# A gated spectral mixer with product-key experts: another source for the tiles of D, rows copied two steps behind their transposes, one store of u, wider score pairs, and one-hots issued one at a time

## The chip, the cores and the metric

The kernel runs on one core of a Trainium2 chip. Its time is the device time of one execution in microseconds (us). Three runs of the kernel before gave 785.18, 786.75 and 787.69; their median is 786.75. One further execution was profiled and took 783.8.

## The reference

There are S = 2048 tokens of D = 640 columns. The result is y = g\*a + (1-g)\*b with a gate g for each token.

```python
g = sigmoid((x * gate_w).sum(-1))
# a: Fourier mixing over both axes, as dense products
ar = x @ Wd_re.T ; ai = x @ Wd_im.T
a  = Ws_re @ ar - Ws_im @ ai                    # 2048 x 2048 by 2048 x 640
# b: H = 32 heads with product keys, E = 16 keys a side, 256 experts
q  = einsum("nd,dhc->nhc", x, w_q)              # two halves of 128
s1 = q[..., :128] @ k1.T ; s2 = q[..., 128:] @ k2.T
#   the two best of s1 and of s2, the two best of their four sums,
#   g2 = softmax over these two
ue, ve = u[top_e], v[top_e]
b  = einsum("nhk,nhk,nhkd->nd", g2, gelu(einsum("nd,nhkd->nhk", x, ue)), ve)
```

All inputs and the output are fp32. The best-two choice needs the scores at nearly full precision.

## The kernel before

**Products in three parts.** TensorE works on pairs of tiles h and l, where h is a value rounded to the fp32r type and l is the rest. `split(f, h, l, eng)` (L128 to L132) makes them: ScalarE copies f to h, and VectorE or GpSimd (the argument `eng`) subtracts h from f. `mm3` (L134 to L138) adds h by h, h by l and l by h in one PSUM bank. Nearly all of TensorE's time goes into such triples.

**The Fourier part.** The program takes the sequence product first: Ws times x, for real and imaginary parts, in four column groups of 512, each with 16 tiles of W down the sequence. One such tile is a *piece*, with five triples for the five blocks of x (`seq_piece`). The order is all of the real part, the imaginary group 2, then 56 units of a fast 2-by-2 scheme for the imaginary groups 0 and 1 (`quad_step`; the units a11, s1, a12, s2, s4, s3, a22, some of which need sums of W and sums of x), and last the imaginary group 3. Together these are the NPC = 152 pieces of the *first product*. Its results go through ST, a ring of five staging tiles, are multiplied by g or -g on VectorE ("gate products", L227, L293, L307), and are stored in `pd`. The *second product* multiplies them by the D-side matrices Wd and by v, in two rounds of 42 steps, by the same kind of scheme. Its right-hand tiles are called DD (h and l of Wd), `ts` (h and l of sums of Wd) and `vs` (v); DD takes the place of WU, the weights of the score stage, in memory.

**W's lead.** Tiles of W are loaded some five pieces ahead (`wf`) and split three pieces ahead into WS, a ring of four pairs: at piece n the program issues the split of piece n+3, whose buffer piece n-1 has used. In the score stage GpSimd makes the subtraction; from N1 on VectorE does.

**The score stage** lies over pieces N0 to N1. There are eight pairs of token tiles, and a pair takes five pieces: `score_half` behind four of them (15 triples that make the 512 score columns of half a tile), `u_pair` behind the last (the products of x with u, a gelu on ScalarE, and the stores into `actd`). After `u_pair` stands `split_xT`, which makes xh and xl of the next pair on ScalarE and GpSimd; there is one pair of buffers for them. Over the same pieces run the sums of W (`sums_load` to `sums_last`, stored in `sd`) and of x (`x_load` to `x_store`, stored in `td`) that the quad units read back.

**Background work.** `Pump` holds generators of small pieces of VectorE work (the choice of the best two, `topk`, L600 to L621, and the experts). Each triple on TensorE calls `run_bg(0.68)`, which adds share x 0.68 us of credit; generators are advanced until the credit is spent, and each yields the microseconds that it used. A negative yield means "nothing now" and sets the credit to zero. Work with a fixed cost elsewhere takes credit away. `space(f, us)` is a second list: its entries are called in turn, each when the given time has passed since the one before. Through it go the *rows*: expert numbers and weights of a token tile are transposed by three DMAs on SP's queue (`load_rows`), and one step later copied into ROWS by ScalarE (`put_rows`, L685; for the last four tiles by GpSimd). `at(n, f)` puts f behind piece n.

**The experts.** For each of 32 *chunks* of tokens VectorE builds one-hot factors from ROWS (`build`: three operations, L821 to L823, of 2048 elements for a group of two chunks, of 1024 for one), TensorE multiplies them (`use`), ScalarE copies the result to `cd` (L830), and for every fourth chunk `cd` is stored in `gd` by two DMAs on ScalarE's queue (L836). The second product reads `gd`. Groups are double up to eight pieces before the end of the first product, and single from there.

**D's tiles.** `load_dd` and `split_dd` load Wd in five parts of two tiles from N1 on, into the buffers of xf, xh and xl, and split the ten tiles into DD on ScalarE and VectorE. Later `load_dt` loads the same rows of Wd again (and v), from 17 pieces before the second product; `make_sums` and `split_sums` make the sums and split them. The two meet in one place, `t_sum`, which lets one sum's h and l overwrite a quarter of DD (n == 3).

What the order of instructions on an engine is, the program writes out itself: it runs under a manual schedule, and an instruction waits only for its operands and buffers. W, rows, sums and D's parts are loaded over SP's queue; ScalarE's queue carries the stores of `actd`, `gd`, `pd` and the output; GpSimd's queue loads `tq` (the x side of the quad units) and stores part of `pd`.

## Time and profile before

| | |
|---|---|
| median of three runs | 786.75 us |
| the profiled execution | 783.8 us, span 782.0 us |
| TensorE (PE) busy | 762.8 us, 98% of the span |
| VectorE (DVE) busy | 582.5 us, 74% |
| GpSimd (POOL) busy | 358.8 us, 46% |
| ScalarE (ACT) busy | 304.5 us, 39% |
| mean granted clock of TensorE | 0.995 |

In the trace the score stage runs from about 160 to 430 us and the first product ends at about 622 us. A row of the view of instructions gives the start, the duration, the engine, the line, output and input, and in brackets the time that the instruction waited, with what released it. A row of the view of waits gives the waiting engine and tile, what released it, the total wait, the number of waits and the longest. A row of a window gives its bounds and length, then the busy time of PE, PEld, DVE, ACT and POOL with the number of instructions, then the granted clock, the share of the DMA engines and the GB/s. A row of the grouped view gives line, engine, operation and tiles, the busy time and the mean of one in ns, and the idle time before them. ACTq and SPq are the DMA issues on the queues of ScalarE and SyncE.

### The profile page before, as it was taken

To read this page: it belongs to the slowest core of one execution; us is meant where nothing else is said; L and a number is where in the kernel's file an instruction comes from. 1 tells how busy PE (TensorE), PEld (TensorE's weight loads), DVE (VectorE), ACT (ScalarE), POOL (GpSimd) and SP (SyncE) were. 2 spreads that over 40 slices of the span, in tenths; PEclk is the share of its full clock that TensorE was granted. 3 is DMA by queue.
4 is the path that set the end of the run, shared out by engine and by line. 5 is a ranking of instruction groups with operands and counts; after the bars stand their busy time and mean duration, and the time that the engine had idled before them with its cause. 6 is when DMAs were issued, how large, how long until landed. Compare 5 with 4: busy or idle time off the path is not lost.

```text
span 782.0 us, 12300 instructions
## 1 busy us (share of the span) xinstructions
PE 762.8 (98%) x4568; PEld 612.8 (78%) x4568; DVE 582.5 (74%) x676; ACT 304.5 (39%) x505; POOL 358.8 (46%) x279
## 2 busy tenths in 40 slices
PE   9999999999999989998999999999999999999997
PEld 6777677888888878886888877778778788788886
DVE  7641121398999999999999985878689878748761
ACT  5344323232225342444425454434324543543342
POOL 5433224466755575575755024222003465577253
PEclk9999999999999999999999999999999999999999
DMA  9977996646445555636755579898736687676421
GB/s 346 355 264 192 308 342 209 220 145 199 144 168 167 201 184 175 206 109 203 268 164 163 203 235 266 279 297 254 240 104 209 200 273 235 203 256 215 125 63 69
DMA packets 111453, 165.29 MB, mean 211 GB/s; under 512 B 35040, under 2 KB 50528, under 8 KB 111392
## 3 DMA queue, kind: packets, MB, share of 16 engines
q1 hardware_dynamic: 80656, 136.30, 53.0%
q10 hardware_dynamic: 27088, 15.87, 6.6%
q0 software_dynamic: 3648, 12.32, 4.8%
q8 instruction: 36, 0.59, 0.3%
q14 instruction: 25, 0.20, 0.1%
HBM read 126.17 MB, written 36.71 MB: 208 GB/s over the span
## 4 chain that ended last, share of the span: by engine, by line
PE 64%; DVE 20%; DMA 6%; issue 3%; SPq 2%; POOL 2%; ACT 2%; ACTq 0%; DVEq 0%; POOLq 0%
PE b L136 20%; PE b L137 19%; PE b L138 19%; DVE ew L611 3%; PE b L490 2%; DVE rr L615 2%; DVE mm L609 2%; SPq L677 2%; DVE ew L613 2%; DVE ew L618 2%; DVE sc L620 2%; DMA wf<-in_wsim 1%; DMA gd<-cd 1%; DVE WS L132 1%; DVE ST L227 1%
## 5 line engine op out<-in xcount | busy, mean ns | idle before, releaser
L136 PE MATMUL b<-WS,X 128*128 128x512 f32 x555 | 220.1, 397 | 2.8 <-ACT WS L131 1.3
L137 PE MATMUL b<-WS,X 128*128 128x512 f32 x555 | 217.2, 391 | 2.8 <-DVE WS L132 2.7
L138 PE MATMUL b<-WS,X 128*128 128x512 f32 x555 | 216.5, 390 | 0.0
L132 POOL TENSOR_TENSOR WS<-wf,WS 128x512 fp32r<-128x512 f32 x72 | 108.2, 1509 | 124.1 <-ACT WS L131 113.5
L131 ACT ACTIVATE WS<-wf 128x512 fp32r<-128x512 f32 x152 | 94.0, 628 | 102.3 <-PE b L138 43.1
L136 PEld LDWEIGHTS b<-WS,X 128*128 128x128 f32 x555 | 104.3, 188 | 33.5 <-issue 7.8
L137 PEld LDWEIGHTS b<-WS,X 128*128 128x128 f32 x555 | 104.4, 188 | 24.9 <-DVE WS L132 4.6
L138 PEld LDWEIGHTS b<-WS,X 128*128 128x128 f32 x555 | 104.4, 188 | 22.2
L596 ACT ACTIVATE sc<-b 128x512 f32<-128x512 f32 x32 | 19.5, 609 | 134.9 <-PE b L138 134.9
L132 DVE TENSOR_TENSOR WS<-wf,WS 128x512 fp32r<-128x512 f32 x80 | 53.8, 695 | 23.2 <-ACT WS L131 23.1
L136 PE MATMUL b<-WU,xh 128*128 128x512 f32 x160 | 63.0, 394 | 2.8 <-ACT xh L131 2.8
L138 PE MATMUL b<-WU,xl 128*128 128x512 f32 x160 | 63.2, 395 | 2.3 <-POOL xl L132 2.3
L132 POOL TENSOR_TENSOR WS<-ra,WS 128x512 fp32r<-128x512 f32 x40 | 58.1, 1469 | 15.5 <-ACT WS L131 14.1
L137 PE MATMUL b<-WU,xh 128*128 128x512 f32 x160 | 62.8, 392 | 0.0
L275 POOL DMA_DIRECT2D tq<-td x32 | 17.5, 549 | 85.3 <-PE b L138 46.1
L131 ACT ACTIVATE WS<-ra 128x512 fp32r<-128x512 f32 x56 | 34.9, 631 | 54.8 <-PE b L138 33.4
L132 POOL TENSOR_TENSOR WP<-ra,WP 128x512 fp32r<-128x512 f32 x20 | 32.2, 1624 | 46.0 <-ACT WP L131 44.1
L505 DVE TENSOR_TENSOR WU<-b,WU 128x512 fp32r<-128x512 f32 (+1 forms) x16 | 7.9, 491 | 58.2 <-ACT WU L504 58.2
L611 DVE TENSOR_TENSOR ew<-sc,mm 128x1024 f16<-128x1024 f32 x32 | 49.7, 1552 | 1.1
L609 DVE TENSOR_REDUCE mm<-sc 128x64 f32<-128x1024 f32 x32 | 38.9, 1215 | 13.6 <-ACT sc L596 13.0
L996 DVE TENSOR_TENSOR ra<-ra 128x512 f32<-128x512 f32 x48 | 44.6, 980 | 3.5 <-POOL WP L132 3.2
L615 DVE TENSOR_REDUCE rr<-ew 128x64 f16<-128x1024 f16 x32 | 39.0, 1219 | 1.0
(161 smaller groups left out, 1453.7 us busy)
## 6 DMA issues: line engine op xcount, KB each, us to landing
wq<-in_wq SPq DMA_DIRECT2D x32, 640.0 KB, 7.1
ra<-pd SPq DMA_DIRECT2D x70, 256.0 KB, 3.9
wf<-in_wsre SPq DMA_DIRECT2D x63, 256.0 KB, 5.2
wf<-in_wsim SPq DMA_DIRECT2D x56, 256.0 KB, 4.4
sa<-in_wsim SPq DMA_DIRECT2D x32, 256.0 KB, 3.0
sd<-sa SPq DMA_DIRECT2D x32, 256.0 KB, 2.0
tq<-td POOLq DMA_DIRECT2D x32, 256.0 KB, 5.3
wf<-sd SPq DMA_DIRECT2D x32, 256.0 KB, 4.6
```

The lines of the kernel that those rows point to most:

```text
L131: nc.scalar.activation(h, f, AF.Copy)
L132: eng.tensor_sub(l, f, h.bitcast(F32))
L136: nc.tensor.matmul(o, wh, ah, start=first, stop=False, skip_group_check=more)
L137: nc.tensor.matmul(o, wh, al, start=False, stop=False, skip_group_check=more)
L138: nc.tensor.matmul(o, wl, ah, start=False, stop=last, skip_group_check=more)
L275: nc.gpsimd.dma_start(t.bitcast(F32), td[k, :, ("s1", "s3", "a22", "s2").index(what)])
L490: nc.tensor.matmul(ps[32 * j:32 * j + 32, :HALF], kp[:, 8 * G // H, r, :], w[:, j], start=(r == 0), stop=(r == 1))
L596: nc.scalar.activation(scs[i].rearrange("p h e -> p (h e)")[:, c], ps, AF.Copy)
L609: nc.vector.tensor_reduce(m, sc, op=OP.max, axis=AX.X)
L611: nc.vector.tensor_tensor(eq, sc, m[:, :, None].to_broadcast([P, HH, E]), op=OP.is_equal)
L615: nc.vector.tensor_reduce(r, eq, op=OP.max, axis=AX.X)
L996: nc.vector.tensor_add(take((b, o, k)) if f is not None else raw[b, o, k], raw[b, o, k] if f is None else f, raw[b, what, k])
```

## The change

Five things are different, and some small ones go with them.

1. `load_dd` and `split_dd` are gone. `make_sums` splits DD's h and l out of the tile that `load_dt` has loaded for the sums: one ScalarE copy and one VectorE subtraction of 2 x 640 columns for each of the five tiles. `load_dt` runs a piece later from the third tile on.
2. Rows are copied two steps behind their transposes, with 8 us between steps; for the last four tiles one step behind with 6 us. There are three buffers for `rt`.
3. u's two results are stored by one DMA instead of two. Except where the next piece is the last of its column group, this store is issued behind the next piece, after the split of the next pair's x.
4. A pair of score tiles gets a sixth piece every second time: the stage is 44 pieces long instead of 40.
5. The three operations of a one-hot group are yielded singly, so that other work may stand between them. A pause no longer forfeits the credit that is left (up to 2.4 us are kept). A group whose result goes into a fresh `cd` is used 12 us after the issue of the last store into `gd` at the earliest, and while the later buffers don't exist yet, a group is used 8 us after it was built.

Smaller: the h parts of x's sums are stored a piece or two earlier than the l parts; `sd`'s last store stands at the start of the next pair; the gate rows and one result row share a buffer with `sx`; one pair of quad units changes places, so that s2 ends a unit earlier; `tq`'s first loads come a piece later; the credit's share in the quad units and behind is 1.12 instead of 1.1.

```diff
+QUNITS[5 * HN - 3:5 * HN - 1] = QUNITS[5 * HN - 2:5 * HN - 4:-1]
...
             if c is None or c < 0:
-                self.credit = 0.0
+                self.credit = 0.0 if c is None else min(self.credit, 2.4)
...
 def load_rows(a):
-            t = p2.tile([P, 3, P], F16, name="rt", bufs=2)
+            t = p2.tile([P, 3, P], F16, name="rt", bufs=3)
...
+        lag, gap = (1, 6.0) if b == NT // NB - 1 else (2, 8.0)
         def step(a):
             if a < NB:
                 got[a] = load_rows(a)
-            if a:
-                put_rows(a - 1, got.pop(a - 1))
-        for a in range(NB + 1):
-            bg.space(lambda a=a: step(a), 5.0 if a and b == NT // NB - 1 else 8.0)
+            if a >= lag:
+                put_rows(a - lag, got.pop(a - lag))
+        for a in range(NB + lag):
+            bg.space(lambda a=a: step(a), gap)
...
+    def apart(n):
+        return n if pieces[n + 1][2] == NT - 1 else n + 1
 def u_pair(p):
         nc.scalar.activation(act, ps, AF.Gelu_apprx_tanh)
-        for n in range(2):
-            nc.scalar.dma_start(actd[n][:, 2 * p * P:2 * (p + 1) * P], act[:, n])
+        def put_act():
+            nc.scalar.dma_start(actd[:, :, 2 * p * P:2 * (p + 1) * P].rearrange("n p t -> p n t"), act)
+        n = N0 + 5 * p + p // 2 + 4
+        if apart(n) == n:
+            put_act()
+        else:
+            at(n + 1, put_act)
...
     for p in range(NP):
-        n = N0 + 5 * p
+        n = N0 + 5 * p + p // 2
...
+        at(apart(n + 4), x_high, p)
...
-    N1 = N0 + 5 * NP
-    at(N1, x_store, HN - 1)
+    N1 = N0 + 5 * NP + NP // 2
+    at(N1 - 1, sums_last, HN - 1)
+    at(N1 - 1, x_store, HN - 1)
...
 def build(g, c, s, n, us):
             nc.vector.tensor_tensor(pt, row(0), wt, op=OP.is_equal)
+            yield us
             nc.vector.tensor_tensor(qt, row(1), wt, op=OP.is_equal)
+            yield us
             nc.vector.tensor_tensor(pt, pt, row(2), op=OP.mult)
+            yield us
...
 def use(group):
+            while group[0][1] % 4 == 0 and bg.now < put[0] + 12.0 and not ending:
+                yield -1.0
...
-                    if p3 is None:
-                        yield 3.0
+                    while p3 is None and bg.now < built + 8.0:
+                        yield -1.0
...
-                build(g, c, s, k)
-                yield (1.1 if not last_part else 1.65) * 2 if k == 1 else 3.6
+                yield from build(g, c, s, k, 1.2 if k == 2 else 1.1 if last_part else 0.75)
...
-    def load_dd(m):
-    def split_dd(m, a):
...
 def make_sums(k):
         bg.credit -= 2.3
+        if k < KD:
+            split(f, DD[:, :, 0, k], DD[:, :, 1, k], nc.vector)
+            bg.credit -= 1.5
...
-        at(NPC - 17 + 2 * k, load_dt, k)
+        at(NPC - 17 + 2 * k + (k > 1), load_dt, k)
...
-        share = 0.95 if n < N1 else 1.0 if n < Q0 + 8 else 1.1
+        share = 0.95 if n < N1 else 1.0 if n < Q0 + 8 else 1.12
```

The order that comes of it, at three places. In these rows a number behind x counts equal instructions in a row, and a line number is that of the kernel in question: the split is L131 and L132 before, L134 and L135 in the changed kernel.

ScalarE at the end of the fifth score pair (the gelu of u, L718 before and L731 now, the store of u, the split of the next pair's x), before:

```order
L131 ACTIVATE ST<-sx 128x512 x2
L718 ACT_TABLE_LOAD
L718 ACTIVATE ST<-b_2525 128x512
L720 DMA actd<-ST 128x256 x2
L131 ACTIVATE xh<-xf 128x640 x2
L131 ACTIVATE WS<-wf 128x512 x2
L596 ACTIVATE sc<-b_2626 128x512
```

and of the change:

```order
L134 ACTIVATE ST<-sx 128x512 x2
L731 ACT_TABLE_LOAD
L731 ACTIVATE ST<-b_2561 128x512
L134 ACTIVATE xh<-xf 128x640 x2
L134 ACTIVATE WS<-wf 128x512
L734 DMA actd<-ST 128x2x256
L134 ACTIVATE WS<-wf 128x512
L694 ACTIVATE rows_1188<-rt 128x384
```

The store has moved from ahead of the split of x to behind it and one split of W; at the third and the sixth pair it still stands right behind the gelu.

VectorE in the quad units (one-hots L821 to L823, the split's subtraction into WS, the gate product into `wrow`, an addition L289), before:

```order
L132 TENSOR_TENSOR WS<-wf,WS 128x512 x3
L821 TENSOR_TENSOR hot_4059<-rows_1189,wtab_144 128x2048
L822 TENSOR_TENSOR hot_4059<-rows_1189,wtab_144 128x2048
L823 TENSOR_TENSOR hot_4059<-hot_4059,rows_1189 128x2048
L307 SCALAR_TENSOR_TENSOR wrow<-b_3730,grow 128x512
L289 TENSOR_TENSOR ST<-ST,b_3884 128x512
L132 TENSOR_TENSOR WS<-wf,WS 128x512
```

and of the change, where the one-hots are L847, L849 and L851, the gate product into the shared buffer is L316 and the addition L298:

```order
L135 TENSOR_TENSOR WS<-wf,WS 128x512 x4
L847 TENSOR_TENSOR hot_4144<-rows_1188,wtab_143 128x2048
L849 TENSOR_TENSOR hot_4144<-rows_1188,wtab_143 128x2048
L851 TENSOR_TENSOR hot_4144<-hot_4144,rows_1188 128x2048
L847 TENSOR_TENSOR hot_3567<-rows_1188,wtab_143 128x2048
L135 TENSOR_TENSOR WS<-wf,WS 128x512 x2
L849 TENSOR_TENSOR hot_3567<-rows_1188,wtab_143 128x2048
L851 TENSOR_TENSOR hot_3567<-hot_3567,rows_1188 128x2048
L316 SCALAR_TENSOR_TENSOR rest<-b_3615,rest 128x512
L298 TENSOR_TENSOR ST<-ST,b_3834 128x512
L135 TENSOR_TENSOR WS<-wf,WS 128x512
```

Three one-hots stood ahead of the two result operations before; now there are four one-hots, two splits, two one-hots and then these operations.

VectorE at the end of the first product (the last sums of Wd and v, L943 to L947 before and L942 to L946 now; the splits into `vs` and `ts`; what follows are the operations on `ra` of the second product), before:

```order
L132 TENSOR_TENSOR WS<-wf,WS 128x512
L943 TENSOR_TENSOR tf<-dt 128x512
L944 SCALAR_TENSOR_TENSOR tf<-tf,dt 128x256
L945 TENSOR_TENSOR tf<-tf 128x256
L946 TENSOR_TENSOR tf<-dt 128x256
L947 TENSOR_TENSOR tf<-dt 128x128
L132 TENSOR_TENSOR vs<-dt,vs 128x1280
L132 TENSOR_TENSOR ts<-tf,ts 128x256
L132 TENSOR_TENSOR vs<-tf,vs 128x256
L132 TENSOR_TENSOR ts<-tf,ts 128x128
L1032 TENSOR_SCALAR ra<-ra 128x512
```

and of the change:

```order
L135 TENSOR_TENSOR DD<-dt,DD 128x2x640
L135 TENSOR_TENSOR WS<-wf,WS 128x512
L135 TENSOR_TENSOR ts<-tf,ts 128x256
L135 TENSOR_TENSOR DD<-tf,DD 128x256
L135 TENSOR_TENSOR ts<-tf,ts 128x128
L135 TENSOR_TENSOR WS<-wf,WS 128x512
L851 TENSOR_TENSOR hot_3567<-hot_3567,rows_1189 128x1024
L847 TENSOR_TENSOR hot_3567<-rows_1189,wtab_143 128x1024
```

The subtraction for DD stands ahead of a split of W, and behind the last split of W come one-hots of single groups, the last of them (L849 and L851) behind the splits into `vs` and `ts`.

More of the change, by code (lines that the diff above doesn't have):

```diff
@@ L57, in __init__ @@
         self.clock = 0.0
+        self.now = 0.0
     def space(self, f, us):
@@ L65, in tick @@
         self.clock += us
+        self.now += us
         if self.apart and self.clock >= self.apart[0][1]:
@@ L215, in gated_mix_kernel, with row_tile @@
     p3, last_part, ending, share = None, False, False, 0.95
-    grow, staged = {}, {}
+    grow, staged, rest = {}, {}, []
+    def row_tile(q):
+        if q < NC:
+            return pools[-1].tile([P, TC], F32, name="grow", tag="grow")
+        if not rest:
+            rest.append(pa.tile([P, 2, TC], F32, name="rest", tag="C"))
+        return rest[0][:, 0]
     def load_row(q):
-        grow[q] = pools[-1].tile([P, TC], F32, name="grow", tag="grow")
+        grow[q] = row_tile(q)
         nc.sync.dma_start(grow[q], gdr[q % NC * TC:(q % NC + 1) * TC].partition_broadcast(P))
@@ L319, in q_post @@
         elif what == "a12":
-            f = p3.tile([P, TC], F32, name="wrow")
+            f = rest[0][:, 1]
             at(n, w_out, 0, f)
@@ L731, in x_load @@
     def x_load(k):
-        sa["x"] = p2.tile([P, 2, TC], F32, name="sx")
+        sa["x"] = pa.tile([P, 2, TC], F32, name="sx", tag="C")
         nc.sync.dma_start(sa["x"], xn[k::HN, :, :4 * P].rearrange("a p d -> p a d"))
@@ L758, in x_split, with x_high @@
             split(f, sa["h"][n], f.bitcast(F32R), nc.gpsimd)
+    def x_high(k):
+        for n in range(2):
+            nc.sync.dma_start(td[k, :, 2 * n:2 * n + 2, 0], sa["h"][n].bitcast(F32).rearrange("p (j c) -> p j c", j=2))
     def x_store(k):
@@ L762, in x_store @@
             return
-        for n in range(2):
-            nc.sync.dma_start(td[k, :, 2 * n:2 * n + 2, 0], sa["h"][n].bitcast(F32).rearrange("p (j c) -> p j c", j=2))
         nc.sync.dma_start(td[k, :, :, 1], sa["x"].rearrange("p n (j c) -> p (n j) c", j=2))
@@ L837, in sums @@
                                         cd[g][n::2, :, n, :])
+                put[0] = bg.now
             if c == 15:
@@ L1173, in gated_mix_kernel @@
             bg.add(experts(), late=True)
-        if HOT and p3 is None and len(rowed) == NT and not grow:
+        if HOT and p3 is None and len(rowed) == NT:
             p2_stack.close()
```

40 lines of the change are left out of this document (12 added, 28 removed).

## The prediction

> **What bounds the kernel now.** I read the page first (shares of the engines, granted clock), then the waits of TensorE, then its busy time in stretches of 20 us, and last the instructions around each gap.
>
> ```profile
> PE 762.8 (98%) x4568; PEld 612.8 (78%) x4568; DVE 582.5 (74%) x676; ACT 304.5 (39%) x505; POOL 358.8 (46%) x279
> ```
> ```profile
> PE b L136 <- ACT xh L131: 2.8, 2, 1.6
> PE b L137 <- DVE WS L132: 2.7, 3, 1.4
> PE b L849 <- ACT cd L830: 2.6, 2, 1.9
> ...
> PE b L136 <- DVE ST L309: 1.3, 1, 1.3
> ```
> ```profile
> 280.00:300.00 20.00, 17.38 (x70) 13.59 (x69) 19.48 (x21) 6.86 (x10) 10.07 (x6) 0.91 0.66 219
> 340.00:360.00 20.00, 17.52 (x91) 14.46 (x89) 19.52 (x16) 7.23 (x12) 13.87 (x11) 1.00 0.42 128
> 460.00:480.00 20.00, 18.55 (x142) 14.84 (x142) 12.22 (x19) 6.35 (x11) 7.79 (x10) 1.00 0.95 285
> 480.00:500.00 20.00, 18.48 (x141) 14.43 (x140) 14.71 (x18) 8.62 (x15) 6.36 (x9) 1.00 0.92 277
> 500.00:520.00 20.00, 18.86 (x203) 14.57 (x202) 16.34 (x23) 8.93 (x15) 4.54 (x8) 1.00 0.85 252
> 540.00:560.00 20.00, 18.10 (x255) 14.29 (x254) 14.03 (x16) 5.64 (x11) 3.44 (x6) 0.91 0.80 254
> 560.00:580.00 20.00, 18.71 (x203) 14.76 (x203) 16.78 (x22) 6.33 (x11) 0.55 (x1) 1.00 0.61 179
> 600.00:620.00 20.00, 19.26 (x208) 15.73 (x208) 18.59 (x31) 11.86 (x27) 8.11 (x9) 1.00 0.67 189
> ```
>
> TensorE has work in 98% of the span and the change neither adds nor removes a matmul, so all that can be won is what these rows lack of 20 us: 2.62, 2.48, 1.45, 1.52, 1.14, 1.90, 1.29 and 0.74 us, 13.1 together. Two rows also show a granted clock of 0.91, that is 1.8 us of full-speed work lost in each. The ceiling is thus 16.7 us, or 2.1% of the span. The waits name four different releasers: no single cause is behind it, so I take the gaps one by one.
>
> **The score stage (two gaps).** The rows of ScalarE around them:
>
> ```profile
> 278.05 0.94 ACT L718 ACTIVATE ST<-b 128x512 f32<-128x512 f32 x1
> 281.95 2.15 ACTq L720 DMA_DIRECT2D actd<-ST  x2
> 284.15 1.36 ACT L131 ACTIVATE xh<-xf 128x640 fp32r<-128x640 f32 x2 [5.16 <-DMA wf<-in_wsre]
> ```
> ```profile
> 357.59 1.37 ACT L131 ACTIVATE xh<-xf 128x640 fp32r<-128x640 f32 x2 [6.99 <-DMA actd<-ST]
> ```
>
> The gelu ends at 279.0, but the two stores of u are issued only at 281.95 and 283.8, each after the landing of an earlier transfer, and the split of the next pair's x stands behind them on the same queue. TensorE waits for it. The change issues one store, and in six of eight pairs behind the split and one piece later (its order is shown above); for the other two pairs the store still comes first, but there the transposes lie a step away. Its own wait then holds up only splits of W, which have a lead: the ring is four buffers, so up to three pieces. I count both gaps and the lost clock as won: 2.62 + 2.48 + 1.8 = 6.9. If they stay, nothing of that comes.
>
> A copy of rows, too, waits on that queue now:
>
> ```profile
> L685 ACT ACTIVATE rows<-rt 128x384 f16<-128x384 f16 x12 | 23.4, 1950 | 11.4 <-DMA rt<-gs 11.3
> ```
>
> Two steps behind instead of one, with 8 us between steps, the 11.3 us of waiting should go; they lie beside matmuls in all but the gaps above, so I add nothing for them.
>
> Spreading the pairs over 44 instead of 40 pieces adds no matmul, but it sets what VectorE must do in that stage against more time:
>
> ```profile
> 160.00:430.00 270.00, 264.88 (x1271) 222.69 (x1270) 261.18 (x242) 99.33 (x139) 168.77 (x113) 0.99 0.55 179
> 430.00:570.00 140.00, 133.90 (x1301) 106.45 (x1300) 112.96 (x155) 60.63 (x101) 27.79 (x41) 0.99 0.80 250
> 570.00:622.00 52.00, 49.98 (x463) 40.49 (x462) 47.43 (x78) 21.34 (x48) 14.45 (x16) 1.00 0.56 167
> ```
>
> VectorE is busy 261 of 270 us there. Without the two gaps the stage would be 263 us long and VectorE next to bind; four pieces more (15 matmuls each, one every 0.227 us by the rows of 552 us further down, so 3.4 us a piece) make it 276.7, VectorE at 94%. So the cover for the 6.9 us is the spreading. It is paid for later: the same four pieces no longer stand between the score stage and the products.
>
> **D's parts from the other tiles.** Removed after the score stage: ten loads of 320 KB, ten ScalarE copies, and ten VectorE subtractions.
>
> ```profile
> L132 DVE TENSOR_TENSOR DD<-draw,DD 128x640 fp32r<-128x640 f32 x10 | 8.2, 818 | 0.0
> ```
> ```profile
> 458.31 3.09 DVE L227 SCALAR_TENSOR_TENSOR ST<-ST,grow 128x512 f32<-128x512 f32 x5
> 461.32 0.82 DVE L132 TENSOR_TENSOR DD<-draw,DD 128x640 fp32r<-128x640 f32 x1
> 462.06 0.68 DVE L132 TENSOR_TENSOR WS<-wf,WS 128x512 fp32r<-128x512 f32 x1
> ```
>
> The gap at 461 (1.45) is this: five gate products, then a part of D, then the split that TensorE waits for. Before it stands another part of D. Without them, and with the gate products still in a stretch of whole pieces, 1.45 goes to zero. The work comes back as five subtractions of 1280 columns in the last 14 pieces before the second product; the trace prices them at 8.2 us in all (two of 818 ns each), and their ScalarE copies beside them have room (21.3 of 52 us busy). What it displaces is costed under the end, below.
>
> **One-hots singly, and the new waits in the list of background work.**
>
> ```profile
> 480.91 2.10 ACTq L836 DMA_DIRECT2D gd<-cd  x2
> 483.06 1.09 ACT L286 ACTIVATE ST<-b 128x512 f32<-128x512 f32 x2 [4.05 <-DMA rt<-gs]
> ...
> 554.60 0.60 ACT L830 ACTIVATE cd<-b 128x512 f32<-128x512 f32 x1 [7.53 <-DMA gd<-cd]
> ```
> ```profile
> DMA to landing us min/median/max: 4.5/5.5/11.1
> ```
>
> At 553 the copy into cd waits 7.53 us for the landing of gd, read from the same cd, and the splits of W stand behind it. The change lets a first group be used only 12 us after the issue; the slowest landing took 11.1. So 1.90 goes, and with it the slow clock (1.8): the rows of the matmuls show when it came.
>
> ```profile
> 552.73 0.39 PE L137 MATMUL b<-WS,X 128*128 128x512 f32 x1
> 552.95 0.39 PE L138 MATMUL b<-WS,X 128*128 128x512 f32 x1
> ```
> ```profile
> 556.82 0.63 PE L136 MATMUL b<-WS,tq 128*128 128x512 f32 x1
> 557.25 0.63 PE L137 MATMUL b<-WS,tq 128*128 128x512 f32 x1
> ```
>
> Before the gap one matmul starts every 0.22 to 0.23 us, after it every 0.43, and the idle time between was only 1.90 us; the 2.48 us at 356 left the clock at 1.00, so whether a gap costs clock too is not in its length alone. [...]
>
> At 483 it is gd's issue that waits, 4.05 us, behind a transpose's landing. In the new order the first gd comes after more loads; the background list also pauses there. I take the 1.52 as won; bounds 0 to 1.52.
>
> What one-hots cost in the products is shown by the gap at 507:
>
> ```profile
> 502.83 1.22 DVE L821 TENSOR_TENSOR hot<-rows,wtab 128x2048 f16<-128x2048 f16 x1
> ...
> 507.43 0.69 DVE L132 TENSOR_TENSOR WS<-wf,WS 128x512 fp32r<-128x512 f32 x1
> ```
>
> From 502.83 to 507.43, 4.6 us (three one-hots and two additions), no split comes, and TensorE lacks 1.14 in that slice. The change puts splits between one-hots at most places, but not at this one: the order has four one-hots in a row (4 x 1.14 = 4.6), two splits, then two one-hots and two additions (3.5). The first costs 1.1 again, the second between 0 and 1.8, since the lead is used up; I take 0.9, so this place gets dearer by 0.9. The gap at 572 (1.29, L309 in the waits) keeps a chunk of the same length, three one-hots and two additions; I leave it.
>
> **The end of the first product.** From 570 to 622 VectorE is free for 4.6 of 52 us. The order adds 8.2 of D there, and one-hots for 12.8 instead of 11.0 us (two groups of 3 x 1.22 and three half groups, against three groups): 5.4 more than there is. The lead of up to three pieces takes most of that. But a half group is now used two microseconds before the end of the stage, and its last two one-hots stand behind the last sums: TensorE waits between 0 and 5.4 there; I take 2.0, since VectorE starts the stretch with some pieces in hand. Four single uses instead of one double add 0.5 by my estimate from the 0.74 of the slice that now holds two in a row.
>
> The other edits (x stores a piece earlier, sd's last store a piece later, shared buffers for rows, s2 ending a unit earlier, dt a piece later, share 1.12) move transfers whose landings are not named in the waits; they cost nothing while the lead of the splits holds.
>
> **Sum.** Won 6.9 + 1.45 + 1.52 + 1.90 + 1.8 = 13.6; lost 0.9 + 2.0 + 0.5 = 3.4; net 10.2. The profiled execution took 783.8 us (span 782.0 and 1.8 around it), so 773.6 for one like it. The median of the runs is 786.75, 2.95 above it; with that, 776.5.
>
> **Rivals.** *VectorE sets the pace after the score stage.* From 430 to 622 it is busy 160.4 of 192 us, 83.5%, and loses cover when pieces move forward. If it can't get denser, only the score stage's 6.9 remain, less up to the 3.4: 780 to 783. For it: 47 of 52 at the end; against: 96.7% in the score stage hardly hurt. 0.20.
> *More goes than I count*: the gaps at 507, 572 and 610 as well, 13.6 + 1.14 + 1.29 + 0.74 = 16.8: 770. For it: more splits stand between one-hots. 0.10.
> *The landing waits only change place*: the store of u, or a late copy of rows, still stops ScalarE ahead of what TensorE needs. The 6.9 stay and the 3.4 eat the rest up to 3.3: 783 to 787. Against it: the split now precedes the store. 0.12.
> *Slower: the end is bound by VectorE, with GpSimd beside it.*
>
> ```profile
> 586.54 0.42 DVE L945 TENSOR_TENSOR tf<-tf 128x256 f32<-128x256 f32 x1
> 586.87 0.96 DVE L946 TENSOR_TENSOR tf<-dt 128x256 f32<-128x256 f32 x1
> ```
>
> Like shapes take 0.42 alone and 0.96 beside GpSimd's part of the sums. If all of D's 8.2 stretched so, 10.5 more, the stretch would be 16 us late, and a slow clock 1.8 more: against the 12.2 won elsewhere (13.6 less 0.9 and 0.5) that is 5.5 slower, 792. [...] It decides from a lateness of 14.6 on (12.2 and the 2.4 of a measurable loss). 0.08.
>
> **Chances.** My forecast 0.50, its own range 773 to 780. A measurement tells 0.3% from no change, 2.4 us here. Faster (under 784.4): 0.50 + 0.20 + 0.10, less the upper edge of the second case, 0.03: 0.77. Same: that edge and most of the third rival, 0.14. Slower 0.09. The range that leaves out two in ten or less, from the rival with more to the third rival: 769.5 to 786.
>
> **What would show it.** Right: no wait of TensorE for xh or xl, the clock at full in the slices around 285 and 556, no wait for cd after a gd store. Wrong: waits for WS by VectorE in the last ten pieces, waits of L849's successor for hot, a slow clock at new places. The forecast fails if VectorE's share from the score stage's end to the second product stays at 83.5%.

## The result, and where the time went

The changed kernel takes 776.65 us (median of four runs, 776.48 to 777.08), the kernel before 785.96 (four runs, 784.50 to 787.69). The ratio is 0.9881, with a 95% interval of 0.9859 to 0.9904: faster by 1.2%. On a second chip the same comparison gave 777.97 against 786.17, a ratio of 0.9900 (0.9877 to 0.9923). The forecast was 776.5 with a range of 769.5 to 786.0. Runs over 1.5% slower than the fastest of the same kernel on the same chip are left out of the ratios, here and below; that takes 9 of the 29 runs of the kernel before on the chip of e9 to e12.

The profiled execution of the changed kernel took 777.08 us, its span is 775.3. From its page, the shares of the engines:

```profile
PE 760.8 (98%) x4568; PEld 612.3 (79%) x4568; DVE 577.3 (74%) x673; ACT 303.4 (39%) x502; POOL 367.1 (47%) x283
```

The waits of TensorE (what it waited for, the total, the number, the longest):

```profile
PE b L881 <- ACT cd L859: 3.0, 1, 3.0
PE b L881 <- DVE hot L851: 2.7, 1, 2.7
PE b L140 <- DVE WS L135: 1.2, 1, 1.2
...
PE b L139 <- ACT ST L1130: 0.9, 1, 0.9
```

and the windows of 20 us that answer to those shown of before, with two at the end of the first product:

```profile
280.00:300.00 20.00, 20.00 (x93) 16.68 (x92) 19.48 (x26) 7.03 (x11) 11.38 (x8) 1.00 0.57 188
340.00:360.00 20.00, 19.93 (x103) 16.77 (x102) 18.38 (x14) 11.89 (x17) 18.41 (x12) 1.00 0.43 144
460.00:480.00 20.00, 20.00 (x192) 16.05 (x191) 12.55 (x16) 8.91 (x15) 7.33 (x9) 1.00 0.96 270
480.00:500.00 20.00, 18.68 (x183) 14.66 (x170) 18.93 (x22) 9.03 (x15) 5.78 (x7) 1.00 0.84 272
...
540.00:560.00 20.00, 20.00 (x331) 15.83 (x330) 16.39 (x19) 7.51 (x13) 0.55 (x1) 1.00 0.78 245
...
580.00:600.00 20.00, 17.00 (x192) 13.77 (x191) 17.42 (x32) 11.87 (x23) 4.84 (x5) 0.91 0.60 186
600.00:620.00 20.00, 17.27 (x131) 13.66 (x130) 19.64 (x29) 9.15 (x21) 8.96 (x7) 0.92 0.48 153
```

The waits for xh and xl are gone, and the slices around 290, 350, 470 and 550 us are full (19.93 us or more of 20) at full clock. But at 586 and 613 us stand two waits that are longer than any before, 3.0 and 2.7 us, and both slices show a clock of 0.91 and 0.92. The share of busy time is the same 98% as before: it doesn't tell the two kernels apart.

A table by stage does. For it I took, from the traces, the time from the start of each matmul to the start of the next, less the median of that time for matmuls of the same line and tiles, and summed this excess. It holds both the waits and the slow clock, that is stretches in which the granted clock is 0.5. The stages are bounded by the first and the last matmul that uses xh or xl, the last that uses tq, and the first that uses DD or ts. (All times below that are called an excess come out of this reckoning; the excess of a gap is some 0.2 us more than the wait in the profile.)

| excess of TensorE, us | score stage | quad units | last pieces | second product |
|---|---|---|---|---|
| before | 7.6 | 13.0 | 3.6 | 1.7 |
| before, second trace (e12) | 9.0 | 12.6 | 4.0 | 6.1 |
| changed | 0.7 | 5.1 | 10.3 | 2.7 |
| changed, second trace (e5) | 0.7 | 6.1 | 10.3 | 2.1 |

Between the first traces: 6.8 and 7.9 us won in the score stage and the quad units, 6.8 and 1.0 lost behind them. The sum is 6.9; the start, ahead of the score stage, differs by 0.2 the other way (23.5 before, 23.7 changed), and the spans by 6.7. So the change wins 14.7 us and gives more than half of it back, nearly all in the last pieces of the first product.

### The profile page after: what moved, and what is told of

It reads as the page before. It is cut to its first block, busy times and chain, and to the rows that moved or that the text cites. A ratio compares the mean times of both kernels' runs of the same rounds, so it can differ in the third digit from the quotient of the medians.

```text
span 775.3 us, 12266 instructions
## 1 busy us (share of the span) xinstructions
PE 760.8 (98%) x4568; PEld 612.3 (79%) x4568; DVE 577.3 (74%) x673; ACT 303.4 (39%) x502; POOL 367.1 (47%) x283
## 5 line engine op out<-in xcount | busy, mean ns | idle before, releaser
L135 POOL TENSOR_TENSOR WS<-wf,WS 128x512 fp32r<-128x512 f32 x76 | 112.5, 1486 | 157.7 <-ACT WS L134 134.8
L134 ACT ACTIVATE WS<-wf 128x512 fp32r<-128x512 f32 x152 | 95.2, 629 | 135.1 <-PE b L141 57.9
L135 DVE TENSOR_TENSOR WS<-wf,WS 128x512 fp32r<-128x512 f32 x76 | 51.9, 699 | 18.8 <-ACT WS L134 18.6
L135 POOL TENSOR_TENSOR WS<-ra,WS 128x512 fp32r<-128x512 f32 x40 | 58.4, 1476 | 15.5 <-ACT WS L134 14.8
L135 POOL TENSOR_TENSOR WP<-ra,WP 128x512 fp32r<-128x512 f32 x20 | 32.9, 1659 | 51.5 <-ACT WP L134 51.5
L134 ACT ACTIVATE WS<-ra 128x512 fp32r<-128x512 f32 x56 | 34.8, 630 | 52.9 <-PE b L141 29.1
L998 DVE TENSOR_TENSOR ra<-ra 128x512 f32<-128x512 f32 x48 | 41.9, 921 | 2.2 <-DMA ra<-pd 2.1
```

The lines of the kernel that those rows point to most:

```text
L134: nc.scalar.activation(h, f, AF.Copy)
L135: eng.tensor_sub(l, f, h.bitcast(F32))
L998: nc.vector.tensor_add(take((b, o, k)) if f is not None else raw[b, o, k], raw[b, o, k] if f is None else f, raw[b, what, k])
```

## The two new waits

ScalarE, VectorE and TensorE of the changed kernel around 586 us (start, duration, engine, line, tiles; in brackets the wait and what ended it):

```profile
586.24 1.48 DVE L135 TENSOR_TENSOR DD<-dt,DD 128x1280 fp32r<-128x1280 f32 x1
```
```profile
587.76 0.42 ACT L134 ACTIVATE DD<-tf 128x256 fp32r<-128x256 f32 x1 [2.61 <-DVE DD L135]
...
588.28 0.61 ACT L134 ACTIVATE WS<-wf 128x512 fp32r<-128x512 f32 x1
588.80 0.57 ACT L859 ACTIVATE cd<-b 128x512 f32<-128x512 f32 x1
```
```profile
589.42 0.69 PE L881 MATMUL b<-hot 128*32 128x32 f16 x64 [3.00 <-ACT cd L859]
```

Two groups of one-hots are used right after each other here, in both kernels; the second needs the bank that the copy into cd empties. Before, that cost 0.74 us. Now that copy stands behind the copy of a sum into DD. That sum overwrites 256 of the 1280 columns which VectorE's subtraction reads and writes (a fifth; "a quarter of DD" further up is too much), and this subtraction, new at this place, ends at 587.7. ScalarE waits 2.61 us for it, and TensorE 3.00.

VectorE around 613 us, and TensorE:

```profile
608.52 1.34 DVE L943 SCALAR_TENSOR_TENSOR tf<-tf,dt 128x256 f32<-128x256 f32 x1
609.79 0.96 DVE L944 TENSOR_TENSOR tf<-tf 128x256 f32<-128x256 f32 x1
610.67 0.96 DVE L945 TENSOR_TENSOR tf<-dt 128x256 f32<-128x256 f32 x1
...
611.76 1.48 DVE L135 TENSOR_TENSOR vs<-dt,vs 128x1280 fp32r<-128x1280 f32 x1
...
614.26 0.69 DVE L849 TENSOR_TENSOR hot<-rows,wtab 128x1024 f16<-128x1024 f16 x1
614.87 1.76 DVE L851 TENSOR_TENSOR hot<-hot,rows 128x1024 f16<-128x1024 f16 x1
```
```profile
616.68 0.41 PE L881 MATMUL b<-hot 128*32 128x32 f16 x32 [2.73 <-DVE hot L851]
```

This is the place that the prediction named: the last two one-hots of a single group behind the last sums. VectorE has no pause of more than 0.2 us from 606 us on. It has what was moved here to do, and four of its operations take 2.3 to 3.2 times their usual time: 1.34 and twice 0.96 for operations that took 0.42 at 590 us, 1.76 for the last one-hot against 0.69 for the one before it. Beside all four GpSimd was subtracting (607.47 to 611.35 and 614.49 to 617.76 us). What they lost adds up to 3.1 us, more than the wait of 2.73, so without the stretching there would be no wait. Without the moved work there is none either: in e3 below the operations are stretched alike (1.33, twice 0.95 and 1.78 us), and the one-hot is there in time, at 616.3 us. It takes both.

## The experiments

Each ratio is to runs of the kernel before on the same chip, with its 95% interval; the changed kernel has 0.9881 and 0.9900. Excesses by stage (score stage, quad units, last pieces, second product) are of the profiled execution of each.

### The score stage: the store alone, without it, and without the wider spacing

Two stores right behind the gelu again (e1):

```diff
-        def put_act():
-            nc.scalar.dma_start(actd[:, :, 2 * p * P:2 * (p + 1) * P].rearrange("n p t -> p n t"), act)
-        n = N0 + 5 * p + p // 2 + 4
-        if apart(n) == n:
-            put_act()
-        else:
-            at(n + 1, put_act)
+        for n in range(2):
+            nc.scalar.dma_start(actd[n][:, 2 * p * P:2 * (p + 1) * P], act[:, n])
```

> The changed kernel with the store of u as before: two stores, right behind the gelu of every pair; the wider spacing of the pairs and all else stays. My theory: the order of ScalarE's queue won the score stage's gaps, so they come back, 2.6 and 2.5 us of waits for xh and xl and up to 1.8 of slow clock: 776.6 + 5 to 7 = 781.5 to 783.5. Rival: the wider spacing alone opened them (later landings have more time), then there is no wait for xh and the time stays at 776.6 within 0.7.

779.91 us, ratio 0.9910 (0.9881 to 0.9940). In the score stage the excess is 1.9 instead of 0.7: gaps of 0.8 and 1.0 us, and no wait for xh or xl. The rest of what it is slower lies elsewhere in that execution (quad units 10.8), with two stores of gd that held ScalarE's queue for 5.16 us instead of 1.9: by the trace's records the second waited until 496.18 us, when a load of `wf` landed that had used its semaphore before. So neither side was right as it stood: the store's place and number are worth about 1 us when the other parts are there, not 5 to 7. ScalarE at the end of the fourth pair in e1:

```profile
282.32 0.60 ACT L731 ACTIVATE ST<-b 128x512 f32<-128x512 f32 x1
282.95 0.81 ACTq L734 DMA_DIRECT2D actd<-ST  x2
```

The stores no longer wait, though they stand where they stood before. In e1 the first is issued within 0.04 us of the gelu's end at all eight pairs. In the kernel before it was so at six; at the fourth and the sixth it came 3.0 and 4.2 us later, within 0.1 us of the landing of the last of three transposes of rows (281.88 and 354.75 us). Here too the store waited for the semaphore that it signals itself, and this transpose had used it last. In e1 no transpose is under way at these two pairs: the other edits of the stage have moved them.

Five pieces for every pair again (e2):

```diff
-        n = N0 + 5 * p + p // 2
+        n = N0 + 5 * p
-    N1 = N0 + 5 * NP + NP // 2
+    N1 = N0 + 5 * NP
```

> The changed kernel with five pieces for each pair again (a score stage of 40 pieces); the one late store and all else stays. The prediction called the spreading the cover of the won 6.9 us: then VectorE, 261 us of work in a stage of 263, makes TensorE or the score buffers wait, and 3 to 7 us come back: 779.6 to 783.6. Rival: the store's place won the gaps alone, and the spreading only took four pieces (13.6 us) from VectorE behind the stage; then the waits at the end of the first product (for one-hots, 2.7 us with 1.8 of slow clock behind it) shrink or go: 772 to 775.5.

777.98 us, ratio 0.9889 (0.9857 to 0.9922), which is no difference from the changed kernel. The windows of the score stage, then the two behind it:

```profile
160.00:413.00 253.00, 253.00 (x1229) 214.28 (x1228) 242.78 (x232) 93.11 (x133) 172.15 (x112) 1.00 0.57 181
413.00:557.00 144.00, 141.06 (x1338) 112.56 (x1337) 119.62 (x157) 60.36 (x97) 35.28 (x43) 0.99 0.80 238
557.00:618.00 61.00, 58.67 (x498) 47.91 (x497) 54.69 (x85) 30.56 (x60) 17.21 (x18) 0.97 0.52 163
```

TensorE is busy in all of 253 us with VectorE at 96%: the wider spacing is not the cover of the score stage's gain. As the rival had it, the last pieces lose less without it (4.5 instead of 10.3). But the quad units lose 9.3 (with one wait of 2.4 us for the landing of tq) and the second product 6.7. The sum stays: 43.6 us of excess over all stages and the start, against 42.5 and 43.1 in the two traces of the changed kernel.

The late single store alone, in the kernel before (e11):

```diff
-        for n in range(2):
-            nc.scalar.dma_start(actd[n][:, 2 * p * P:2 * (p + 1) * P], act[:, n])
+        def put_act():
+            nc.scalar.dma_start(actd[:, :, 2 * p * P:2 * (p + 1) * P].rearrange("n p t -> p n t"), act)
+        n = N0 + 5 * p + 4
+        if pieces[n + 1][2] == NT - 1:
+            put_act()
+        else:
+            at(n + 1, put_act)
```

> The kernel before with one part alone: one store of u, behind the split of the next pair's x and one piece later (at the third and sixth pair right behind the gelu); no wider spacing, rows and D as before. The prediction's term for this part is 6.9 us (2.62 and 2.48 of waits, 1.8 of slow clock): 786.2 - 5.1 to 6.9 = 779.3 to 781.1. Rival: without the spreading VectorE, 261 of 270 us busy there, takes the gain back: 783 to 786.

782.10 us, ratio 0.9963 (0.9929 to 0.9998). By the absolute time that is between the two forecasts. By the ratio it is 2.9 us faster than the kernel before (0.2 to 5.6; the runs that the ratio uses have a mean of 784.9, not 786.2), which is the rival's price and not my 5.1 to 6.9. The gaps at 283 and 356 us are gone, but a new one stands one pair later than the second, and the stage has 6.9 us of excess in all. ScalarE there, and TensorE:

```profile
376.94 2.23 ACTq L238 DMA_DIRECT2D pd<-ST  x2
379.23 0.60 ACT L596 ACTIVATE sc<-b 128x512 f32<-128x512 f32 x1 [7.93 <-DVE ST L227]
...
387.31 1.28 ACT L718 ACT_TABLE_LOAD   x1 [5.46 <-DMA pd<-ST]
```
```profile
389.88 0.50 PE L136 MATMUL b<-WU,xh 128*128 128x512 f32 x1 [2.52 <-ACT xh L131]
```

The gelu writes into a staging tile of ST and waits for a store into pd to land; that store was issued only at 376.9, when the gate products were done; ScalarE stood idle for 7.93 us there, 2.23 of them for the issue of two stores. With the store of u out of the way, the next thing on the same queue stops the same split. In the changed kernel this didn't happen, with (0.7) or without (-0.1 in e2) the wider spacing. What e2 has and e11 lacks are the rows two steps behind and the other edits of that stage; which of them is the one wasn't tried. At the sixth pair of e11 the store of u still waits until a transpose has landed (350.7 us), but the split of x stands ahead of it now, at 346.9. For the two gaps of the kernel before, then, either is enough: the store behind the split with the transposes where they were (e11), or the transposes elsewhere with the store where it was (e1).

### D's parts: loaded first again, and split without the columns that are overwritten

D loaded and split behind the score stage, as before the change (e3):

```diff
+    for m in range(3):
+        at(N1 + m, load_dd, m)
+    for m in range(KD):
+        for a in range(2):
+            at(N1 + 3 + 2 * m + a, split_dd, m, a)
+        at(N1 + 4 + 2 * m, load_dd, m + 3)
...
-        if k < KD:
-            split(f, DD[:, :, 0, k], DD[:, :, 1, k], nc.vector)
...
-        at(Q0 + TSTEPS[j - 6] if j >= 6 else Q0 + 2 + j, load_t, j)
+        at(Q0 + TSTEPS[j - 6] if j >= 6 else Q0 + 4 + j, load_t, j)
```

> The changed kernel with D's ten tiles loaded and split right behind the score stage again, as before; tq's first loads stand two pieces later so that the buffers are free. My theory of single gaps: the gap of 1.45 us behind the gate products comes back, and both waits at the end of the first product (3.0 us for the copy into cd, 2.7 us for a one-hot, 1.8 of slow clock behind each) go, since VectorE has 8.2 us less to do there: 776.6 + 1.5 - 9.3 = 768.8 (767.5 to 771). Rival, VectorE as the pace: the 8.2 us only change place and come back as waits for WS among the quad units: 775 to 779.

780.84 us, ratio 0.9911 (0.9880 to 0.9943); the profiled execution took 777.34. My 768.8 is wrong. The median is above the rival's 775 to 779 too, but the rival describes the trace: the last pieces lose 6.1 instead of 10.3, the quad units 9.2 instead of 5.1, and the sum over all stages and the start is 42.4, as in the changed kernel (42.5). The waits of TensorE:

```profile
PE b L881 <- ACT cd L859: 3.8, 3, 2.8
PE b L140 <- DVE WS L135: 2.6, 3, 1.6
PE b L139 <- ACT DD L134: 2.2, 1, 2.2
```

The third row is at 462 us. ScalarE there:

```profile
455.42 0.64 ACT L134 ACTIVATE WS<-wf 128x512 fp32r<-128x512 f32 x1 [2.89 <-DMA wf<-in_wsim]
...
461.43 0.63 ACT L134 ACTIVATE WS<-wf 128x512 fp32r<-128x512 f32 x1 [3.59 <-DMA wf<-in_wsim]
```

Its splits of W waited for W's landing, while D's ten tiles were loaded over the same queue. The subtractions for DD took VectorE 7.4 us at the end of the changed kernel. Without them the wait for a one-hot is gone, but a wait of 2.8 us stands at 616 us, now for a copy into cd that waits for the landing of gd. That the new source for D wins anything by itself is not shown beyond the uncertainty.

D split in three parts that leave out the 256 columns which the sum overwrites (e4):

```diff
-            split(f, DD[:, :, 0, k], DD[:, :, 1, k], nc.vector)
+            for n, c in ((slice(0, 2), slice(0, 2 * P)), (1, slice(2 * P, 4 * P)), (slice(0, 2), slice(4 * P, D))):
+                split(f[:, n, c], DD[:, n, 0, k, c], DD[:, n, 1, k, c], nc.vector)
```

> The changed kernel, with D split in three pieces that leave out the 256 columns which the split of a sum overwrites a little later; the result needs none of them. Theory: at 586 us ScalarE's copy of that sum waits 2.61 us for VectorE's subtraction over all 1280 columns, and the copy into cd, which frees the bank that TensorE waits for, stands behind it. Without the overlap that wait goes: TensorE's 3.0 us fall to about 0.7 as in the kernel before (0.74), and its 1.8 us of slow clock go: 772.5 (771.5 to 774). Rival: VectorE is late there in any case and the copy into cd waits for something else of it: 775.5 to 777.

774.54 us, ratio 0.9840 (0.9815 to 0.9865): faster than the kernel before beyond doubt, and faster than the changed kernel by its second comparison (0.9877 to 0.9923), while the interval of the first (0.9859 to 0.9904) just touches. ScalarE and TensorE at the same place:

```profile
585.60 0.42 ACT L134 ACTIVATE DD<-tf 128x256 fp32r<-128x256 f32 x1 [0.46 <-DVE tf L945]
...
587.08 0.58 ACT L859 ACTIVATE cd<-b 128x512 f32<-128x512 f32 x1
```
```profile
587.71 0.66 PE L881 MATMUL b<-hot 128*32 128x32 f16 x64 [0.84 <-ACT cd L859]
```

VectorE has about the same work at the same time (1.35 us in three operations instead of 1.48 in one, from 586.24 on), and still ScalarE no longer waits for it. TensorE waits 0.84 us instead of 3.00, and the clock stays at 1.00 there (the window of 580 to 600 us). The first new wait is shown to be the overlap of the two tiles' columns, not VectorE's load. The time is 2 us above my 772.5. The other wait grew (an excess of 3.2 instead of 2.9), and the kernel before is 1.3 us slower on this chip (787.28) than on the one from which I had reckoned.

### One-hots: in threes again, and without the 12 us

The three operations of a group together again (e6):

```diff
             nc.vector.tensor_tensor(pt, row(0), wt, op=OP.is_equal)
-            yield us
             nc.vector.tensor_tensor(qt, row(1), wt, op=OP.is_equal)
-            yield us
             nc.vector.tensor_tensor(pt, pt, row(2), op=OP.mult)
-            yield us
+            yield 3 * us
```

> The changed kernel with the three operations of a one-hot group yielded as one again; the credit kept and the two new waits stay. If single yields won the gaps at 507 and 572 us (1.16 and 1.45), and took the cover at the end, then these come back and the end keeps its cost: 778 to 780. Rival: the end's waits are made by single yields (the first of two one-hots of a group ahead of the sums, the other two behind), and in threes they shrink: 771 to 775.

779.73 us, ratio 0.9918 (0.9899 to 0.9936). This is inside my forecast. Quad units 9.9 instead of 5.1 to 6.1, last pieces 8.2 instead of 10.3. The gap at 572 us doesn't come back; at 495 stand six one-hots in a row (489.5 to 497.4) and a gap of 2.45 us. In this trace both theories got their half: singles win about 4 us in the quad units and cost about 2 at the end; by the intervals (they overlap with both of the changed kernel's) the two kernels are not clearly apart.

Without the wait after a store into gd (e7):

```diff
-            while group[0][1] % 4 == 0 and bg.now < put[0] + 12.0 and not ending:
-                yield -1.0
```

> The changed kernel without the 12 us between the issue of a store into gd and the next group that goes into a fresh cd; the computation is whole. My step: the landing holds ScalarE's copy again, TensorE waits about 1.9 us once (the gap before at 553) and the clock falls for 1.8 us: 776.6 + 3.7 = 780.3 (778 to 782). Rival: with single yields a group is late enough anyway, and groups that come earlier relieve the end: 772 to 777.

779.82 us, ratio 0.9907 (0.9884 to 0.9930), not apart from the changed kernel. The time is inside my forecast, but by luck: its step did not come. No wait of the kind of 553 us comes back: groups stand elsewhere in this order. The wait for the copy into cd is now at 606 us with 3.6 us, again behind a copy into DD that waits 2.60 us for VectorE. So it is not shown that the 12 us by themselves win anything: without them the order changes, and the old wait stays away.

### The end: no one-hots in the last pieces, and what takes their place

e4's split, and `share` at zero from four pieces before the end (e8):

```diff
-        share = 0.95 if n < N1 else 1.0 if n < Q0 + 8 else 1.12
+        share = 0.95 if n < N1 else 1.0 if n < Q0 + 8 else 1.12 if n < NPC - 4 else 0.0
```

> The changed kernel with D split without the 256 columns that are overwritten (as in e4_dd_skip), and without new one-hots in the last four pieces of the first product: they go into the second product, where VectorE is busy some 70%. If the wait for a one-hot at 613 us (2.7 us, and the slow clock behind it) comes from VectorE being late by its last sums there, it goes: 774.5 - 4.8 = 769.7 (768.5 to 771.5). Rival: three groups more in the second product make waits of their own there (ScalarE's splits behind VectorE's additions, as at 647 us): 772 to 776.

777.44 us, ratio 0.9893 (0.9867 to 0.9919). The time is above both forecasts. The wait for the one-hot is gone as expected: the last pieces lose 1.8 instead of 10.3. But the second product loses 9.3 instead of 2.7, 5.1 of it in one gap of 3.6 us and its slow clock, at 641 us. Then with the second `make_z` two steps later (e9), and with the credit forfeited at a pause (e10):

```diff
-        for n, i, j in ((0, -4 if b else -3, -1), (1, 4, 8)):
+        for n, i, j in ((0, -4 if b else -3, -1), (1, 4, 10)):
```
```diff
-                self.credit = 0.0 if c is None else min(self.credit, 2.4)
+                self.credit = 0.0
```

> As e8_skip_hold, but the second of the two make_z in each half of the second product is issued two steps later, behind three of VectorE's additions for s2 and s3 that don't need it. If the wait that replaced the one-hot's (TensorE 3.4 us at 641 us, for ScalarE's copy of W, behind a split that waits for such an addition, behind make_z that waits for the landing of gd's rows) is made by that order, it goes with its slow clock (1.6): 777.4 - 5 = 772.4 (771 to 774). Rival: VectorE stays late and the wait goes to the next place: 775.5 to 778.

> As e9_hold_z, and a pause in the list of background work forfeits its credit, as in the kernel before. In the order the four one-hots in a row among the quad units are then gone: a split of W stands between most of them. If those four make the gap at 496 us (1.35 to 2.5 us in five traces), it goes: 1.5 to 2.5 us less than e9_hold_z, without counting a slow clock there. Rival: the gap there comes from the two result operations and the gate products alone, and stays: within 1 us of e9_hold_z.

781.66 us, ratio 0.9962 (0.9935 to 0.9990), and 784.69, ratio 1.0004 (0.9976 to 1.0032): worse, against both sides of either forecast. The last pieces lose 2.0 and 1.3 us, the second product 14.2 and 18.1. In e9 the additions no longer wait behind `make_z` but for their own loads:

```profile
637.50 0.69 DVE L999 TENSOR_TENSOR ra<-ra 128x512 f32<-128x512 f32 x1 [9.90 <-DMA ra<-pd]
```

Where that may come from is on SyncE's queue. In the changed kernel, the chain of waits and the queue (start, duration, what):

```profile
631.65 5.12 DMA pd<-ST
636.78 0.32 SPq L1028
```
```profile
626.83 10.28 SPq L1028 DMA_DIRECT2D ra<-gd  x4
...
637.68 1.80 SPq L1028 DMA_DIRECT2D ra<-gd  x4
639.58 9.82 SPq L994 DMA_DIRECT2D ra<-pd  x11
```

The last results of the first product go through VectorE's gate products into pd. By the chain of waits (the profile infers its links) a load of gd stood at the head of the queue until that store had landed, at 636.8, and the loads of pd behind it. That is 16 us after the start of the second product, 18.6 in e8 and e9, and the additions come later still.

The matmul that is held up is the same one each time, 26 to 27 us of TensorE's work behind the start of the second product. Since the chain begins with the last results of the first product, TensorE doesn't outrun it by coming sooner or later: it waits when the chain takes longer than that. The matmul came 27 us behind the start in the changed kernel (a wait of 0.9) and some 30 in e8 and in the second trace of before (3.4 each). Why it is longer in e8, where VectorE has less to do before it, I can't say from these rows.

In e10 four one-hots in a row no longer stand among the quad units; the gap at 495 us is 1.4 as before. ScalarE's splits waited for W's landings there, up to 4.25 us. So that gap doesn't need the four. The later losses of e9 and e10 have one more size that I can show but not explain: two subtractions into WP on GpSimd at 661 us took 6.97 us together, 3.5 each against a mean of 1.66 in the changed kernel, and TensorE waited 4.1 us for them. VectorE was at work on additions without a break beside them.

### Second traces of both kernels

> The changed kernel, unchanged, beside the others on one chip: 776.6 within 1.5. The two waits at the end of the first product (2.9 and 3.2 us with about 1.8 us of slow clock behind each) are made by the order of the program, so they should be in this execution too. Rival: they belong to one execution, as the length of a gap before (2.5 at 356 us) that kept its clock suggests, and this trace shows others.

777.97 us, ratio 0.9900 (0.9877 to 0.9923). The two new waits are there again, 2.4 and 3.3 us in excess, each with slow clock behind it, and the last pieces lose 10.3 in both: the waits are the program's.

> The kernel before, for a second trace. The prediction added 2.95 us for the distance of the runs' median from the profiled execution, without a cause. If that is slow clock behind gaps that are there in any case, this execution shows the same eight gaps at 283, 356, 461, 483, 507, 553, 572 and 610 us and, if it takes 786 or more, more stretches of slow clock than the two of the first trace. Rival: its gaps themselves are longer or others.

One execution of 789.47 us (span 787.7). Its waits:

```profile
PE b L136 <- ACT xh L131: 3.8, 2, 2.7
PE b L136 <- ACT ST L1128: 3.4, 1, 3.4
```

All eight gaps are there, at the same places within 4 us, and seven of them within 0.5 us of the first trace; that at 356 us is 1.3 us longer and now has the slow clock that it lacked, while those at 283 and 553 have none. Most of the rest is a ninth wait, 3.4 us at 657 us with 1.4 of slow clock, the one of the second product just described. So the rival held: the distance between these two executions is mostly another gap. The granted clock is 0.996, no lower than the 0.995 of the shorter execution.

## Why the prediction was right, point by point

The time is right (776.65 for 776.5), but so near only by luck, for two errors cancel: the gain of one execution over another was put 3.5 us too high (10.2, measured 6.7), and the constant for the median 3.4 too high (2.95, where the changed kernel's median lies 0.4 below its profiled execution).

- **Score stage, 6.9.** Measured 6.8. The working behind it was partly wrong. "The cover for the 6.9 us is the spreading" fell with e2. The store behind the split does take away the two gaps (e11), but it is not needed for that (e1), and alone it brought 2.9 us, since the stop moved to another instruction of the same queue.
- **Rows, nothing added.** The waits of ScalarE's copies of rows did go, from 11.4 to 3.3 us:

```profile
L694 ACT ACTIVATE rows<-rt 128x384 f16<-128x384 f16 x12 | 23.4, 1953 | 3.3 <-DMA pd<-ST 3.3
```

- **D's gap at 461 (1.45), gd's issue at 483 (1.52), cd at 553 (1.90 and 1.8).** All four went: no wait in the slices from 460 and 540 on, clock at 1.00. The gap at 572 (1.29), which I left, went too, and the one at 507 came back as 1.2 at 497 us, where I had reckoned 1.14 and 0.9 more. Together the quad units won 7.9, where the sum had 6.7 less 0.9.
- **The end, 2.0 and 0.5 for single uses.** This term is the mis-sized one: 6.8 measured, and 1.0 more in the second product, for which I had nothing. The wait for the one-hot was 2.7 where I took 2.0, inside its bounds of 0 to 5.4. What was missing is the slow clock behind it (1.7: 3.41 us at half clock) and the whole of the wait at 586 with its own slow clock: I had priced the subtractions for DD as time of VectorE, but not as something that a copy on ScalarE's queue waits for, ahead of the copy into cd. The rows for it were there: the double use at 610 us with its 0.74, and `t_sum`, which writes into DD.
- **2.95 for the distance of the median from the profiled execution.** It was added without a cause. e12 shows what such a distance can be: a wait at about 657 us that not every execution has. From median to median the gain is 9.3 us, more than the 6.7 of the two profiled executions, because the trace of before was one of the shorter ones.
- **Rivals.** "VectorE sets the pace after the score stage" had 0.20. Its signs came. VectorE (the third busy time) of the changed kernel in the quad units and in the last pieces, from the last use of tq to the second product, and of the kernel before in the last pieces:

```profile
425.00:553.00 128.00, 126.68 (x1161) 102.24 (x1160) 107.69 (x143) 57.63 (x91) 31.65 (x44) 1.00 0.80 253
553.00:621.00 68.00, 62.27 (x595) 49.91 (x593) 63.07 (x96) 31.86 (x63) 18.57 (x18) 0.95 0.54 171
```
```profile
569.00:629.00 60.00, 57.98 (x539) 47.17 (x527) 52.13 (x85) 25.55 (x56) 17.18 (x18) 1.00 0.58 176
```

In the last pieces that is 93% against 87%, and in e2, e3, e8, e9 and e10 what was won in one stage came back in another. Its price (780 to 783) did not come, for the gaps of the quad units went as well. The slower rival named GpSimd beside VectorE's sums at the end: operations of VectorE were stretched there (1.76 against 0.69), by 3.1 us ahead of the wait for the one-hot. But D's subtractions, for which the rival reckoned 10.5, were not stretched at all: the five took 1.48 us each, which is less than the 1.64 that the prediction allowed.

```profile
L135 DVE TENSOR_TENSOR DD<-dt,DD 128x1280 fp32r<-128x1280 f32 x5 | 7.4, 1483 | 2.4 <-ACT DD L134 2.4
```

- **What would show it.** Of the signs named for right, all three came; of those for wrong, the wait for hot and the slow clock at new places came too, the waits for WS in the last ten pieces did not. VectorE's share from the score stage's end to the second product did not stay at 83.5%: it is 87% (107.69 and 63.07 of 196 us). Naming places rather than only a total is what let the trace sort this out.

## What to carry to other kernels

When a kernel that is bound by one engine loses a little at many places, a gain at one can be met by the next wait on the same queue, as in e11 (2.52 us, one pair later): after removing one, look for what stands behind it on that queue and for the next landing on the way to the end, and price a moved operation also as something that others wait for. Where a later operation overwrites part of an earlier one's output, try leaving that part out: here it added no work (1.35 us of VectorE instead of 1.48), took ScalarE's wait of 2.61 us for VectorE away and gave the fastest kernel of all tried (774.54 us). And take two traces of the kernel before, since a distance between two executions can be a wait that one of them doesn't have.

## What the runs showed of the hardware

The length of a gap alone did not tell whether slow clock came behind it. In the first trace of before the clock was 0.50 behind the gap of 1.90 us at 553, where a matmul started every 0.43 us instead of every 0.22 to 0.23, and stayed at 1.00 behind the 2.48 at 356. In the changed kernel it was 0.50 behind the waits of 3.00 and 2.73 us; in e3 it stayed at 1.00 behind one of 2.80.

Leaving out the end, the records of the granted clock in the first traces of the two kernels have two stretches at 0.5 each, and all four are 3.41 us long. Their starts are 269.65 us apart in the kernel before and 27.31 in the changed one, which is 79 and 8 times 3.413. So I laid each trace out in slots of 3.413 us that start where these stretches start, and took the idle time of TensorE in each. The slots just ahead of the four had 2.32 and 1.90 us (at 283 and 553 before) and 2.93 and 2.70 (at 586 and 613 in the changed kernel). Of the others, behind the first 10 us and ahead of the last 10, none had more than 1.59. That one is at 356 before: the gap there lies in two slots, with 1.59 and 0.90 us idle. The changed kernel at its wait of 2.73 us, and e3 at its wait of 2.80, in stretches of that length:

```profile
613.24:616.65 3.41, 0.71 (x4) 0.23 (x2) 3.26 (x6) 2.90 (x7) 2.16 (x2) 1.00 0.90 283
616.65:620.07 3.42, 3.39 (x39) 2.78 (x40) 3.42 (x5) 1.07 (x3) 1.11 (x1) 0.50 0.76 194
```
```profile
614.12:617.53 3.41, 2.33 (x20) 1.70 (x10) 3.41 (x4) 1.11 (x2) 1.85 (x2) 1.00 1.07 261
617.53:620.95 3.42, 1.70 (x38) 1.45 (x38) 2.89 (x5) 2.14 (x6) 0.53 (x1) 1.00 0.61 159
620.95:624.36 3.41, 3.41 (x17) 2.82 (x16) 3.38 (x5) 2.20 (x5) 2.32 (x2) 1.00 1.00 370
```

The first wait lies in one slot (2.70 us idle) and the next has half the clock. The second, no shorter, is parted between two (1.08 and 1.72), and the clock stays at 1.00. So of two waits of about the same length one cost clock and the other did not, and what differs in these rows is where they lay; what makes the clock fall they don't show. A stretch of 3.41 us at a clock of 0.50 cost 1.7 us of work at full speed.
